# Blank rows written job by job, a last scatter pinned ahead of a loop, and input loads moved to ACT's queue: a scan and mixture-of-experts kernel

## The chip, the cores and the metric

The kernel runs on one core of one Trainium2 chip. The metric is device time in microseconds (us) for one execution of the whole program; lower is better. Engines are named as the profile names them: PE (TensorE matmul), PEld (its weight load), DVE (VectorE), ACT (ScalarE), POOL (GpSimd) and SP (SyncE); an added q (SPq, POOLq) is the engine's instruction queue.

## The reference

The input is x and f_logit of 4 sequences by 3648 steps by 256 channels. A gated scan comes first, then each of the 14592 tokens is routed to one of 16 experts and passes through its two matrices.

```python
sig = 1.0 / (1.0 + np.exp(-f_logit))
f = lower_bound + (1.0 - lower_bound) * sig
for t in range(S):
    h = f[:, t] * h + (1.0 - f[:, t]) * x[:, t]     # y[:, t] = h
g_idx = argmax(y @ w_group)                          # 4 groups
e_idx = argmax(y @ w_expert[g_idx])                  # 4 experts in each
ye = np.maximum(y @ w1[g, e], 0.0) @ w2[g, e]        # 256 -> 1024 -> 256
out[token] = g_w * e_w * ye                          # softmax weights of the two choices
```

## The kernel before, in words

**Phase 1** cuts the 14592 tokens into 29 units of 512. `p1_load` (L157) brings the inputs of a unit (tile `zt`, 1 MB, 4 buffers) from `in_zx_dram`, two units ahead (`AHEAD` = 3); all these loads stand on SP's queue (L169). `p1_ta` (L172) has ACT compute the gate (tanh at L179, scale and bias at L183), `p1_tb` (L187) has DVE run the scan into `h` (L196, L207), PE transposes `h` into rows (L226) and multiplies with the router's weights (L238), and ACT copies both out (`rows` at L228, `rs` at L241). `route_thunks` (L252) finds the expert of each token and its place in the expert's list for groups of two units; POOL then scatters the rows (L322, 114 indirect DMAs of 128 rows) into the DRAM tensor `xs`, which holds one list for each expert.

**Phase 2** is 32 jobs. Sixteen jobs of kind A take the first two to six tiles (128 tokens each) of every list as soon as these are filled (table `EARLY`); they run between the steps of phase 1. Sixteen of kind B take what is left of the lists, the longest list first; they start when all tokens are routed. A job loads its rows (`job_rows`, L592, tile `xr`, load at L607), its weights in four pieces of 512 KB (`job_weights`, L612, tile `st`, 5 buffers, L615), splits each weight into two halves of 16 bits (`job_split`, L618: ACT's cast at L621 makes `wh`, DVE's subtract at L622 makes `wl`), transposes the rows (L636), and runs two matrix products of three matmuls each (`m1_step`, L655, with ACT at L671 and DVE at L672 behind it; `m2_step`, L675). ACT scales the result by the token's weight (`o`, L687) and POOL scatters it to the output (L688, 123 indirect DMAs).

**The order of the work.** PE, ACT, DVE and POOL are ordered by a scheduler that goes through the program as it is written; SP is under `manual_schedule` (L707) and keeps the order of the text up to `in_order.close()` (L823). The main loop (L795) writes a job's steps and between them, through `bg_step` (L772), the steps of phase 1 and the preparation of the next job. `fetch_to` (L723) keeps the weight loads five pieces ahead. `order()` (L446) closes phase 1: it ranks what is left of the lists (`nord` rows from place `pord` on), and writes 256 blank rows behind each of the 16 lists (L486 to L489), so that a job that reads past the end of a list finds rows that belong to no token. Each blank write is a read of the place from the tile `taili` (L487) and a DMA of 258 KB (L488), all on SP's queue.

**The end.** Behind the last `m2_step` (L821) the count of tiles that did not fit the jobs is read (`left`, L824), and a loop of that many rounds does them (L825); in the execution shown here it makes no round (123 output scatters for the 55 and 68 tiles of the A and B jobs).

Of the kernel before, what the change touches and what calls it, by code (L numbers as in the profile page):

```python
# [15 lines left out]
ALU = mybir.AluOpType  # L16
AX = mybir.AxisListType.X

P = 128
NE = 16  # L20
# [12 lines left out]
O_BUFS = 5  # L33
X_BUFS = 4
AHEAD = 3


@with_exitstack
def gated_scan_moe(ctx: ExitStack, tc, zx, lower, wroute, wexp, out, S):
    nc = tc.nc  # L40
    sync = nc.sync
    ctx.enter_context(nc.allow_low_precision(reason="whole numbers small enough to be exact"))
    N, D = out.shape
# [3 lines left out]
    NT = N // P  # L47
    PRE = max(n for _, n in EARLY) * P
    LW = PRE + N + 2 * P
    LIST = NE * LW  # L50
    LROWS = LIST + 2 * P
    RW = D + 2

    xs = nc.dram_tensor("xs", [LROWS, RW], I32).ap()
# [45 lines left out]
    for u in sorted({u for u, _ in EARLY}):  # L100
# [4 lines left out]
                                scalar1=-1.0, scalar2=None, op0=ALU.add)  # L105
# [12 lines left out]
    blank = const.tile([P, RW], I32, name="blank")  # L118
# [19 lines left out]
    runoff = const.tile([P, NE], F32, name="runoff0")  # L138
    nc.vector.tensor_scalar(out=runoff, in0=eoff, scalar1=-1.0, scalar2=None, op0=ALU.add)
    state = {"runoff": runoff, "h": None}  # L140

    def unit_range(u):
        return u * UNIT, min(N, (u + 1) * UNIT)
# [11 lines left out]
    last_load = {}  # L155

    def p1_load(u):  # L157
        if u >= NU:
            return
        a, b = unit_range(u)  # L160
        w = b - a
        zt = p1.tile([P, 2, KD, UNIT], F32, name="zt", bufs=4)
        src = zx[u * P:(u + 1) * P, :].rearrange("p (s k w) -> p s k w", s=2, k=KD)
        if u == 0:
            for k in range(KD):
                for q in range(2):
                    nc.sync.dma_start(out=zt[:, q, k, 0:w], in_=src[:, q, k, 0:w])
        else:
            last_load[u] = nc.sync.dma_start(out=zt[:, :, :, 0:w], in_=src[:, :, :, 0:w])  # L169
        units[u] = {"z": zt}  # L170

    def p1_ta(u):  # L172
# [158 lines left out]
    def p1_thunks(us, groups):  # L331
# [21 lines left out]
        def put(f):  # L353
            th.append(f or (lambda: None))
            if hasattr(f, "mark"):
                marks[f.mark] = len(th)

        put(lambda: [p1_load(u) for u in range(us[0], us[0] + AHEAD - 1)])
        put(lambda: p1_ta(us[0]))
        for u in us + [us[-1] + 1]:  # L360
            seq = []
            if u in us:
                seq += [lambda u=u: (p1_load(u + AHEAD - 1), u + 1 in us and p1_ta(u + 1), early_blanks(u + 4))]
            if u - 1 in us:
# [78 lines left out]
    regs = {}  # L443
    early_loads = []

    def order():  # L446
        V = nc.vector
        run = const.tile([P, NE], F32, name="run")
# [20 lines left out]
        nord = const.tile([P, NE], F32, name="nord")  # L469
# [4 lines left out]
        pord = const.tile([P, NE], F32, name="pord")  # L474
# [7 lines left out]
        V.tensor_copy(ordi, eord)  # L482
        regs["ordi"] = ordi
        taili = const.tile([1, NE], I32, name="taili")
        V.tensor_scalar(out=taili, in0=state["runoff"][0:1], scalar1=1.0, scalar2=None, op0=ALU.add)
        for e in range(NE):  # L486
            r = sync.value_load(taili[0:1, e:e + 1], min_val=e * LW + PRE, max_val=e * LW + PRE + N)  # L487
            sync.dma_start(out=xs[bass.ds(r, 2 * P), :].rearrange("(p k) c -> p k c", k=2),  # L488
                           in_=blank[:, None, :].broadcast_to([P, 2, RW]))  # L489
        over = const.tile([P, NE], F32, name="over")  # L490
        V.scalar_tensor_tensor(out=over, in0=nord, scalar=63.5, in1=caps, op0=ALU.add, op1=ALU.subtract)
        V.tensor_scalar(out=over, in0=over, scalar1=1.0 / P, scalar2=None, op0=ALU.mult)
# [38 lines left out]
        left = const.tile([1, 1], F32, name="left")  # L531
# [60 lines left out]
    def job_rows(j):  # L592
        e = job_e(j)
        queue = sync
        if j.kind == "A":
            pos = queue.value_load(j.pos[0:1, e:e + 1], min_val=e * LW + PRE - j.tiles * P, max_val=e * LW + PRE)
        elif j.kind == "B":
            pos = sync.value_load(regs["pordi"][0:1, j.idx:j.idx + 1], min_val=0,
                                  max_val=(NE - 1) * LW + 2 * PRE)
        else:  # L600
            pos = sync.value_load(regs["tabs"][0:1, 3 * j.idx + 1:3 * j.idx + 2], min_val=0, max_val=LIST)
        if j.kind != "A":
            job_mask(j)
        j.rows, j.meta = [], []
        for t0, m in j.pieces:
            r = mo.tile([P, 2, RW], I32, name="xr", bufs=XR_BUFS)
            ld = queue.dma_start(out=r[0:j.w, 0:m], in_=xs[bass.ds(pos + t0 * j.w, m * j.w), :].rearrange("(p k) c -> p k c", k=m))  # L607
            if j.kind == "A":
                early_loads.append(ld.ins)
            j.rows.append(r)  # L610
# [95 lines left out]
    in_order = ExitStack()  # L706
# [12 lines left out]
    def bg_to(n):  # L719
        while done[0] < n:  # L720
            bg_pop()
# [28 lines left out]
    def start_macro(mi):  # L750
        mac = macros[mi]
        bg_to(marks[EARLY[mac[0].idx][0]] if mac[0].kind == "A" else marks["order"])
        for j in mac:
            if j.kind != "A":
                job_rows(j)

    def work(mac):
        return sum(len(j.chunks) * KF + j.tiles for j in mac)
# [36 lines left out]
    for mi, mac in enumerate(macros):  # L795
# [5 lines left out]
        left = sum(len(j.chunks) * KF + j.tiles for j in mac)  # L801
# [15 lines left out]
        while q:  # L817
            q.popleft()()
    pj, pc = pending
    for t in range(pj.chunks[pc][1]):  # L820
        m2_step(pj, pc, t)  # L821

    in_order.close()  # L823
    left = nc.values_load(regs["left"][0:1, 0:1], min_val=0, max_val=NT)  # L824
    with tc.For_i(0, left, 1) as it:  # L825
        ent = mo.tile([1, 3], I32, name="ent")
        rem = mo.tile([P, 1], F32, name="rem")
# [2 lines left out]
        j = make_job("X", 0)  # L830
# [54 lines left out]
```

## Time and profile before

| | us |
|---|---|
| median of 3 runs | 883.24 |
| the 3 runs | 876.09, 883.24, 884.25 |
| the profiled execution, its own time | 878.25 |
| its span, first to last instruction | 876.5 |

PE is busy for 753.8 us of the span (86%), DVE for 535.7, ACT for 464.2, POOL for 286.9. The span falls into three parts: up to about 411 us phase 1 and the A jobs run together; from 421 us on the B jobs run alone; the last 10 us close the program. "Granted clock" is the share of TensorE's full clock that the chip allowed in a stretch. A number in brackets behind an instruction is the time that its engine was idle ahead of it, with the instruction or transfer that ended the wait.

### The profile page before, as it was taken

Reading aid. Unit: us, or ns where it says so; the run is one execution under the profiler, and the core shown is the slowest. Engines: PE = TensorE matmul, PEld = TensorE weight load, DVE = VectorE, ACT = ScalarE, POOL = GpSimd, SP = SyncE. Lnnn points to the kernel's source line nnn. Section 1 sums busy time; section 2 is a strip of 40 time slices with the busy share of each in tenths; the row PEclk is TensorE's granted clock in tenths of the full one; section 3 lists DMA queues with packets and bytes.
Section 4 is the critical chain, followed back from the end, with each engine's and each line's share of the span. In section 5 each row is a group of like instructions: output and inputs, shape, how many; then the busy total and the mean of one; then the engine's idle time right before and its main releaser. Section 6 shows DMA issues by size and latency. Waiting matters only on the chain.

```text
span 876.5 us, 17542 instructions
## 1 busy us (share of the span) xinstructions
PE 753.8 (86%) x6629; PEld 646.5 (74%) x6629; DVE 535.7 (61%) x1159; ACT 464.2 (53%) x808; POOL 286.9 (33%) x255
## 2 busy tenths in 40 slices
PE   3452869878887888897799999999999999999995
PEld 2231748756676776766599998999888999999895
DVE  7996959888965953672534454543656445555630
ACT  6763949588745644342545444544555445555531
POOL 0484554734634425541121121212221221112122
PEclk9665979979999989999799999999999999999998
DMA  8993999799897244247641632343543424444300
GB/s 309 273 362 124 304 295 360 225 354 323 279 255 256 101 162 161 100 163 200 223 151 43 217 105 71 105 129 90 144 138 98 122 94 150 146 151 135 126 24 22
DMA packets 59056, 155.34 MB, mean 177 GB/s; under 512 B 11179, under 2 KB 24560, under 8 KB 55515
## 3 DMA queue, kind: packets, MB, share of 16 engines
q1 hardware_dynamic: 44443, 124.12, 44.3%
q0 software_dynamic: 14240, 30.06, 9.8%
q8 instruction: 52, 0.85, 0.4%
q14 instruction: 33, 0.27, 0.1%
q10 hardware_dynamic: 288, 0.03, 0.0%
HBM read 112.65 MB, written 42.05 MB: 176 GB/s over the span
## 4 chain that ended last, share of the span: by engine, by line
PE 56%; issue 11%; DVE 9%; DMA 7%; ACT 4%; SPq 2%; POOL 2%; POOLq 0%; another core or an unknown queue 0%; DVEq 0%; ACTq 0%
PE ps_m L683 9%; PE ps_m L681 9%; PE ps_m L682 9%; PE ps_m L666 8%; PE ps_m L668 8%; PE ps_m L667 8%; DMA st<-in_wexp_dram 5%; DVE wl L622 3%; PE ps_p L636 2%; DVE hl L672 2%; ACT wh L621 2%; POOL out_dram L688 1%; SPq L488 1%; PE ps_p L238 1%; DVE h L207 1%
## 5 line engine op out<-in xcount | busy, mean ns | idle before, releaser
L688 POOL DMA_INDIRECT out_dram<-o,meta x123 | 140.9, 1146 | 472.9 <-ACT o L687 441.2
L681 PE MATMUL ps_m<-wh,hh 128*128 128x256 f16 (+6 forms) x984 | 272.6, 277 | 2.0 <-ACT o L687 1.1
L682 PE MATMUL ps_m<-wl,hh 128*128 128x256 bf16 (+6 forms) x984 | 272.4, 277 | 0.8 <-issue 0.8
L683 PE MATMUL ps_m<-wh,hl 128*128 128x256 f16 (+6 forms) x984 | 272.2, 277 | 0.9 <-issue 0.9
L666 PE MATMUL ps_m<-xh,wh 128*128 128x256 f16 (+12 forms) x896 | 252.7, 283 | 19.8 <-DVE hl L672 19.3
L672 DVE SCALAR_TENSOR_TENSOR hl<-ps_m,hh 128x512 bf16<-128x512 f32 (+11 forms) x270 | 166.1, 620 | 168.7 <-ACT hh L671 128.2
L668 PE MATMUL ps_m<-xh,wl 128*128 128x256 f16 (+12 forms) x896 | 252.4, 283 | 0.2 <-issue 0.2
L667 PE MATMUL ps_m<-xl,wh 128*128 128x256 bf16 (+12 forms) x896 | 252.4, 283 | 0.0
L671 ACT ACTIVATE hh<-ps_m 128x512 f16<-128x512 f32 (+11 forms) x270 | 146.7, 546 | 129.2 <-PE ps_m L668 112.1
L622 DVE TENSOR_TENSOR wl<-st,wh 128x1024 bf16<-128x1024 f32 x128 | 155.4, 1219 | 57.7 <-ACT wh L621 57.5
L322 POOL DMA_INDIRECT xs<-rows,posi x114 | 143.8, 1262 | 110.6 <-issue 27.7
L621 ACT CAST wh<-st 128x1024 f16<-128x1024 f32 x128 | 132.8, 1044 | 43.3 <-DMA st<-in_wexp_dram 22.8
L687 ACT ACTIVATE o<-ps_m,meta 128x256 f32<-128x256 f32 (+6 forms) x123 | 58.3, 474 | 159.5 <-PE ps_m L683 137.7
L681 PEld LDWEIGHTS <-hh 128*128 128x128 f16 (+6 forms) x984 | 112.5, 114 | 12.0 <-issue 4.1
L683 PEld LDWEIGHTS <-hl 128*128 128x128 bf16 (+6 forms) x984 | 112.4, 114 | 10.1 <-issue 2.3
L682 PEld LDWEIGHTS <-hh 128*128 128x128 f16 (+6 forms) x984 | 112.5, 114 | 9.4 <-issue 1.4
L667 PEld LDWEIGHTS <-wh 128*128 128x128 f16 x896 | 88.9, 99 | 38.0 <-issue 22.7
L666 PEld LDWEIGHTS <-wh 128*128 128x128 f16 x896 | 89.0, 99 | 19.1 <-issue 2.7
L668 PEld LDWEIGHTS <-wl 128*128 128x128 bf16 x896 | 88.8, 99 | 19.1 <-issue 1.7
L642 DVE TENSOR_TENSOR xl<-ps_p,xh 128x512 bf16<-128x512 f32 (+9 forms) x68 | 41.9, 617 | 65.1 <-ACT xh L641 64.5
L207 DVE TENSOR_TENSOR_SCAN h<-zt,h 128x512 f32<-128x512 f32 (+4 forms) x56 | 65.1, 1170 | 1.6 <-PE ps_p L226 1.4
L636 PE MATMUL ps_p<-ident,xr 128*128 128x128 f32 (+6 forms) x246 | 40.0, 284 | 30.0 <-DMA xr<-xs 22.0
(120 smaller groups left out, 506.4 us busy)
## 6 DMA issues: line engine op xcount, KB each, us to landing
st<-in_wexp_dram SPq DMA_DIRECT2D x128, 512.0 KB
zt<-in_zx_dram SPq DMA_DIRECT2D x27, 1024.0 KB
xr<-xs SPq DMA_DIRECT2D x31, 258.0 KB
xs<-blank SPq DMA_DIRECT2D x22, 258.0 KB
xr<-xs SPq DMA_DIRECT2D x8, 249.9 KB
out_dram<-o,meta POOLq DMA_INDIRECT x123
xs<-rows,posi POOLq DMA_INDIRECT x114
xs<-blank SPq DMA_DIRECT2D x3, 516.0 KB
```

Of the source, the lines that this page charges most:

```text
L322: sc = nc.gpsimd.indirect_dma_start(out=xs_v[G["t0"] + t][:, :], out_offset=bass.IndirectOffsetOnAxis(ap=R["posi"][:, t:t + 1], axis=0), i ...
L621: nc.scalar.copy(j.wh[i], j.st[i])
L622: nc.vector.tensor_tensor(out=j.wl[i], in0=j.st[i], in1=j.wh[i], op=ALU.subtract)
L666: nc.tensor.matmul(po, w1_at(j.wh, k, c), xh[:, k], start=(k == 0), stop=False)
L667: nc.tensor.matmul(po, w1_at(j.wh, k, c), xl[:, k], start=False, stop=False)
L668: nc.tensor.matmul(po, w1_at(j.wl, k, c), xh[:, k], start=False, stop=(k == KD - 1))
L671: nc.scalar.activation(hi, pv, AF.Relu)
L672: nc.vector.scalar_tensor_tensor(out=j.hl[ch][:, cs[0]:cs[-1] + 1, 0:w], in0=pv, scalar=0.0, in1=hi, op0=ALU.max, op1=ALU.subtract)
L681: nc.tensor.matmul(pm[0:p, 0:D], j.hh[ch][:, c, ts], w2_at(j.wh, c), start=(c == 0), stop=False)
L682: nc.tensor.matmul(pm[0:p, 0:D], j.hh[ch][:, c, ts], w2_at(j.wl, c), start=False, stop=False)
L683: nc.tensor.matmul(pm[0:p, 0:D], j.hl[ch][:, c, ts], w2_at(j.wh, c), start=False, stop=(c == KF - 1))
L688: nc.gpsimd.indirect_dma_start(out=out_v[out_n[0]][:, :], out_offset=bass.IndirectOffsetOnAxis(ap=lt[0:p, r, 0:1], axis=0), in_=o[0:p], in ...
```

## The change

There are three edits. The blank rows behind list number 0 (in the order of the B jobs) are written in `order()`; those of list s + 1 are written by `start_macro` right behind the row loads of B job s, and the place comes from `pord` + `nord` in place of `runoff` + 1. From unit 9 on the input loads are issued from ACT's queue. POOL keeps the order of the text from the last `m2_step` on, and the read of `left` stands inside that stretch.

```diff
+ZX_SP = 9
...
-            last_load[u] = nc.sync.dma_start(out=zt[:, :, :, 0:w], in_=src[:, :, :, 0:w])
+            last_load[u] = (nc.sync if u < ZX_SP else nc.scalar).dma_start(out=zt[:, :, :, 0:w], in_=src[:, :, :, 0:w])
...
+    def tail_blank(s):
+        r = sync.value_load(regs["taili"][0:1, s:s + 1], min_val=PRE, max_val=(NE - 1) * LW + PRE + N)
+        sync.dma_start(out=xs[bass.ds(r, 2 * P), :].rearrange("(p k) c -> p k c", k=2),
+                       in_=blank[:, None, :].broadcast_to([P, 2, RW]))
...
-        V.tensor_scalar(out=taili, in0=state["runoff"][0:1], scalar1=1.0, scalar2=None, op0=ALU.add)
-        for e in range(NE):
-            r = sync.value_load(taili[0:1, e:e + 1], min_val=e * LW + PRE, max_val=e * LW + PRE + N)
-            sync.dma_start(out=xs[bass.ds(r, 2 * P), :].rearrange("(p k) c -> p k c", k=2),
-                           in_=blank[:, None, :].broadcast_to([P, 2, RW]))
+        V.tensor_tensor(out=taili, in0=pord[0:1], in1=nord[0:1], op=ALU.add)
+        regs["taili"] = taili
+        tail_blank(0)
...
             if j.kind != "A":
                 job_rows(j)
+                if j.kind == "B" and j.idx + 1 < NE:
+                    tail_blank(j.idx + 1)
...
     pj, pc = pending
+    in_order.enter_context(tc.manual_schedule(engines={mybir.EngineType.Pool}))
     for t in range(pj.chunks[pc][1]):
         m2_step(pj, pc, t)
-
+    left = nc.values_load(regs["left"][0:1, 0:1], min_val=0, max_val=NT)
     in_order.close()
-    left = nc.values_load(regs["left"][0:1, 0:1], min_val=0, max_val=NT)
```

The first place is SP's queue at `order()`. Before, it ends with the last of the sixteen blank writes (`taili` read, DMA from `blank`), the table for the leftovers (`tab`), and then the weight loads of the next job (`st`):

```order
L487 TENSOR_LOAD taili
L487 ISA x2
L488 ISA
L488 DMA xs<-blank 256x1x258
L522 DMA tab<-resi 128x3
L615 DMA st<-in_wexp_dram 128x1024 x4
L574 TENSOR_LOAD ordi
```

In the changed kernel the same place (its lines are some numbers further down) reads, from the last row load of an A job on:

```order
L611 DMA xr<-xs 128x516
L448 TENSOR_LOAD taili
L448 ISA x2
L449 ISA
L449 DMA xs<-blank 256x1x258
L526 DMA tab<-resi 128x3
L619 DMA st<-in_wexp_dram 128x1024 x4
L578 TENSOR_LOAD ordi
```

One blank write is left of sixteen. The other fifteen stand further down, each between the row loads of one B job and the weight loads that follow, as here:

```order
L611 DMA xr<-xs 124x258
L448 TENSOR_LOAD taili
L448 ISA x2
L449 ISA
L449 DMA xs<-blank 256x1x258
L578 TENSOR_LOAD ordi
L578 ISA x2
L619 ISA
L619 DMA st<-in_wexp_dram 128x1024
```

The second place is ACT's queue in the middle of phase 1, about 170 to 190 us into the program before. The rows before are the tanh of unit 19 with what stands around it (`zt` a unit's input, `hh` the first product of a job, `rs` and `rows` copies for the router):

```order
L621 CAST wh_2279<-st 128x1024
L687 ACTIVATE o<-ps_m_2213,meta 128x256
L228 COPY rows<-ps_p 128x2x256
L179 ACTIVATE zt<-zt 128x1024
L671 ACTIVATE hh<-ps_m_2256 128x2x256
L183 ACTIVATE zt<-zt,mid,half 128x512 x2
L671 ACTIVATE hh<-ps_m_2295 128x2x256
L621 CAST wh_2312<-st 128x1024
L241 COPY rs<-ps_p 128x128
```

The same tanh in the changed kernel:

```order
L691 ACTIVATE o<-ps_m_2177,meta 128x256
L170 DMA zt<-in_zx_dram 128x2048
L180 ACTIVATE zt<-zt 128x1024
L691 ACTIVATE o<-ps_m_2213,meta 128x256
L184 ACTIVATE zt<-zt,mid,half 128x512 x2
L229 COPY rows<-ps_p 128x2x256
L675 ACTIVATE hh<-ps_m_2256 128x2x256
L625 CAST wh_2273<-st 128x1024
L625 CAST wh_2279<-st 128x1024
```

The load now stands ahead of the tanh of the unit before it, and there is one such pair for each unit; the casts of the weights have moved behind the tanh.

The third place is the end of POOL's queue. Before, the last output scatter stands behind the loop (the one at the third row is the loop's own):

```order
L825 UNCONDITIONAL_BRANCH
L881 BRANCH_PREFETCH_HINT
L688 DMA out_dram<-o,meta 14592x256
L825 REGISTER_ALU
L825 COMPARE_AND_BRANCH
L825 UNCONDITIONAL_BRANCH
L688 DMA out_dram<-o,meta 14592x256
L881 UNCONDITIONAL_BRANCH
L881 ISA
```

Now only the loop's own scatter is left there, and the run of scatters ahead of the read of `left` has 91 in place of 90:

```order
L692 DMA out_dram<-o,meta 14592x256 x91
L829 TENSOR_LOAD lefti
L831 COMPARE_AND_BRANCH
L831 ISA
L831 UNCONDITIONAL_BRANCH
L831 ISA
L831 UNCONDITIONAL_BRANCH
L887 BRANCH_PREFETCH_HINT
L692 DMA out_dram<-o,meta 14592x256
L831 REGISTER_ALU
L831 COMPARE_AND_BRANCH
L831 UNCONDITIONAL_BRANCH
```

## Rows read from the trace of the kernel before

**Rows 1.** Stage, length, busy us of PE, PEld, DVE, ACT, POOL, granted clock, DMA

```profile
160.00:250.00 90.00, 74.94 (x613) 56.49 (x611) 78.91 (x156) 62.99 (x111) 44.37 (x35) 0.92 0.92 304
250.00:300.00 50.00, 38.92 (x356) 32.41 (x355) 33.09 (x71) 29.14 (x53) 20.70 (x16) 0.93 0.68 204
411.00:421.00 10.00, 0.16 (x2) 0.00 (x0) 1.64 (x3) 2.72 (x5) 0.00 (x0) 0.76 0.90 239
421.00:427.00 6.00, 5.89 (x23) 3.05 (x23) 4.08 (x7) 3.27 (x6) 0.00 (x0) 0.55 0.76 264
427.00:866.00 439.00, 437.68 (x3970) 400.22 (x3968) 221.56 (x385) 211.94 (x366) 95.28 (x84) 1.00 0.37 116
```

**Rows 2.** Timeline of ACT and PE behind the order step (start, length, idle before)

```profile
418.28 1.04 ACT L621 CAST wh<-st 128x1024 f16<-128x1024 f32 x1 [9.75 <-DMA st<-in_wexp_dram]
421.11 0.48 PE L666 MATMUL ps_m<-xh,wh 128*128 128x384 f16 x1 [9.94 <-DVE hl L672]
```

**Rows 3.** Timeline of SP's queue around the order step

```profile
384.44 3.93 SPq L607 DMA_DIRECT2D xr<-xs  x6
389.19 20.96 SPq L488 DMA_DIRECT2D xs<-blank  x16
410.90 15.00 SPq L615 DMA_DIRECT2D st<-in_wexp_dram  x8
```

**Rows 4.** Chain that ended last: two transfers (start, length)

```profile
111.86 2.48 DMA xr<-xs
...
864.46 3.63 DMA out_dram<-o,meta
```

**Rows 5.** Timeline of SP's queue: two input loads, with what stands ahead of one

```profile
161.05 1.84 SPq L607 DMA_DIRECT2D xr<-xs  x2
163.89 0.42 SPq L169 DMA_DIRECT2D zt<-in_zx_dram  x1
...
262.79 0.42 SPq L169 DMA_DIRECT2D zt<-in_zx_dram  x1
```

**Rows 6.** Timeline of ACT: three tanh steps that waited for their input load

```profile
175.34 1.06 ACT L179 ACTIVATE zt<-zt 128x1024 f32<-128x1024 f32 x1 [3.68 <-DMA zt<-in_zx_dram]
271.13 1.06 ACT L179 ACTIVATE zt<-zt 128x1024 f32<-128x1024 f32 x1 [4.07 <-DMA zt<-in_zx_dram]
281.74 1.06 ACT L179 ACTIVATE zt<-zt 128x1024 f32<-128x1024 f32 x1 [6.35 <-DMA zt<-in_zx_dram]
```

**Rows 7.** Timeline of PE: three gaps between 170 and 290 us

```profile
181.54 0.69 PE L636 MATMUL ps_p<-ident,xr 128*128 128x128 f32 x2 [8.05 <-ACT rs L241]
266.01 0.48 PE L249 MATMUL ps_p<-ident,rs 128*128 128x128 f32 x1 [4.62 <-ACT rs L241]
286.26 0.19 PE L284 MATMUL ps_p<-scn,tri 128*128 128x16 bf16 x1 [4.02 <-DVE xl L642]
```

**Rows 8.** What SP's queue waited for: total us, times, longest; and L169's waits

```profile
SPq L615 <- DVE wl L622: 256.6, 53, 16.3
SPq L607 <- DMA xs<-rows,posi: 53.3, 12, 9.8
SPq L169 <- DVE h L207: 25.7, 6, 5.8
...
L169 SPq EVENT_SEMAPHORE  x11: 17/3426/5729, 5.2 to 47.8; - x11
```

**Rows 9.** Two stretches of the first half, columns as in rows 1

```profile
155.00:161.00 6.00, 6.00 (x68) 5.19 (x67) 6.00 (x16) 4.74 (x8) 4.78 (x5) 1.00 0.23 83
165.00:210.00 45.00, 35.83 (x300) 27.41 (x298) 36.26 (x71) 30.74 (x52) 25.34 (x21) 0.89 1.01 345
```

**Rows 10.** The end: timeline of ACT and POOL; instructions of the closing line

```profile
866.31 0.47 ACT L687 ACTIVATE o<-ps_m,meta 128x256 f32<-128x256 f32 x1 [2.15 <-PEq L825]
869.96 1.00 POOL L688 DMA_INDIRECT out_dram<-o,meta  x1 [4.32 <-issue]
...
L881 POOLq DRAIN  x3: 40/109/5956, 869.7 to 876.2; - x3
```

## The prediction

> **What bounds the kernel now.** I first read busy time by stage. From 427 to 866 us PE is busy for 437.68 of 439.00 us at a granted clock of 1.00 [rows 1]: the B jobs are bound by PE, and nothing that SP, ACT or POOL does there can shorten them; it can only move their start and lengthen the close behind them. So a gain must come from ahead of 427 us or from the last 10 us. Ahead of it PE has room: 74.94 of 90.00 us from 160 on, 38.92 of 50.00 from 250 on, and 0.16 of 10.00 from 411 on [rows 1].
>
> Then I read who ends these gaps. The one at 411 us is plain: PE waits 9.94 us behind DVE's `hl`, but ACT, ahead of DVE, sat 9.75 us with a weight cast that waited for its `st` load [rows 2]. SP issued that load only at 410.90, because sixteen blank writes held its queue for 20.96 us from 389.19 on [rows 3]. It landed 7.4 us later, when the cast began.
>
> The gaps between 170 and 290 us are less plain. Three of them, 8.05, 4.62 and 4.02 us, end on ACT's `rs` and on DVE [rows 7]. ACT stood still shortly ahead of each, at the tanh of a unit whose input had not landed: 3.68, 4.07 and 6.35 us [rows 6]. These inputs are loads that SP issued late. That of unit 19 went out at 163.89, behind a row load of 161.05 [rows 5], and SP's row loads wait for scatters for 53.3 us in all [rows 8]. It was used at 175.34 [rows 6], 11.5 us later; that of unit 26, out at 262.79 [rows 5], at 271.13 [rows 6], 8.3 us later.
>
> The end comes last: the last `o` is done at 866.78 (866.31 and 0.47), but POOL's scatter of it starts at 869.96 [rows 10], behind the empty loop.
>
> **The change part by part: blank rows.** Sixteen writes take 20.96 us, 1.31 us each [rows 3]; fifteen leave this place, 19.65 us. That would let the `st` load go at 391.25. The one write that stays is a write at a place known only at run time, so it has to wait for the six row loads in front of it. The last of those is out at 388.37 (384.44 and 3.93) [rows 3], and a row load took 2.48 us to land [rows 4], so the write goes at 390.9 in place of 389.19 and the load at about 393.0. With the 7.4 us of before it lands at 400.4. ACT asks for it at 408.53 (418.28 less 9.75) [rows 2], so 8.1 us of margin are left and the whole gap of 9.94 us goes.
>
> What is behind the gap goes too. From 421 to 427 us the granted clock was 0.55, after 10 us in which PE had done nothing; from 427 on it was 1.00 [rows 1]. The work of those 6.0 us takes 6.0 x 0.55 = 3.3 us at the upper level (2.4 GHz, against 1.2): 2.7 us. Together 12.6 us. Bounds: 8 us if a later load, say that of the next weights, keeps a third of the gap; 12.6 if nothing does.
>
> The fifteen writes come back among the B jobs. Each costs SP about 1.3 us and a wait until the row loads of its job have landed, 2.5 us by rows 4 and at most the 9.8 us of the longest wait for `xs` [rows 8]. Behind it on SP stand the weight loads of a later job. They are early: SP waited 256.6 us in 53 pieces, 4.8 us each, only for a staging buffer to come free [rows 8], and PE hardly waited from 427 on [rows 1]. I cost this at 0. With that cover gone it would be 15 x 3.8 = 57 us of SP time, which PE would see in part; four such waits, one for each weight piece of a job, are 19 us, so the cover holds even for 1.3 + 9.8 us.
>
> **The pinned scatter.** Now it starts about 0.3 us behind ACT, as other scatters do, at 867.1 in place of 869.96 [rows 10]: 2.9 us earlier. The loop's entry must then wait for it to land, 3.63 us as for the scatter before it [rows 4], 870.7. In the old order POOL went from that landing at 868.09 (864.46 and 3.63) to its closing drain at 869.7, 1.6 us later, and the drain took 5.96 us with the scatter inside, to 875.7 [rows 10]. The new close is thus 870.7 + 1.6 + a drain + 0.8 us (the span ends at 876.5). With an empty drain that is 873.1, a gain of 3.4 us; with a drain as long as before it is 879.1, a loss of 2.6. The nearer row is the drain with work in it, which should shorten once there is none: I take a gain of 3.0, and keep -2.6 to 3.4.
>
> **Input loads from ACT.** Twenty loads (units 9 to 28) leave SP's queue. Each now stands one unit ahead on ACT. Units 19 and 26 are seven apart and their tanhs 95.8 us [rows 6], so a load has some 13.7 us to land where it took 8.3 to 11.5: the three waits of 14.1 us [rows 6] mostly go. Behind them lie PE gaps of 8.05 + 4.62 + 4.02 = 16.7 us [rows 7]. I take half, 8 us, for three reasons: an issue costs its queue about 0.42 us [rows 5], so ACT pays 20 x 0.42 = 8.4 us, in a stretch where DVE is busy for 78.91 of 90.00 us [rows 1] and can't follow a faster PE far; the scatters that SP waited for stay where they are; and the weight loads still stand behind them. Bounds: 20 us (all three gaps and some 3 us of low clock behind them) and -4 us (no gap goes, half of the 8.4 us is seen).
>
> Can the DMA engines take the loads earlier at all? From 165 to 210 us they are busy for 1.01 of the time and a load moved there gains nothing; from 155 to 161 us, while SP waits, for only 0.23 [rows 9]. The Trainium skill, "DMA: Bandwidth & Descriptors", section "Issuing engines are not separate DMA queues", says that transfers of all issuing engines share the same 16 DMA engines and that a second issuer saves only the time of issuing, which is usually small. By that rule alone the edit would be worth about the 8.4 us of SP issue, none of it on PE's path, and the sum would be 862.7; the trace agrees on the sharing (1.01), but shows that an issue here can also be stuck behind a wait.
>
> **The sum**, against the profiled execution's own 878.25: 878.25 - 12.6 - 3.0 - 8.0 = 854.7. That execution lies 5.0 us under the median of the three runs shown, 883.24; the mean of all four is 880.5, 2.2 us above it. I add that: 857 us.
>
> **Rivals.** *The transfer is hidden anyway.* The DMA engines are the limit up to 250 us (0.92 from 160 on [rows 1]), so loads that go out earlier only slow the weight loads beside them, and the first half keeps its length. For it speaks 1.01 [rows 9], against it the 0.23 and the share of 0.68 from 250 on [rows 1], where two of the three waits lie. Then only blanks and end count: 878.25 - 15.6 = 862.7, with the 2.2 about 865.
>
> *ACT takes over SP's waits* (the slower side). SP waited 25.7 us in 6 pieces for DVE to free an input buffer, 4.3 us each [rows 8]. On ACT such a wait holds the casts, the Relu of the first product and the scaled outputs behind it, so PE and DVE stand too. Were each of the sixteen loads from unit 13 on held for 4.3 us and half of it seen by PE, that is 34 us: 878.25 - 15.6 + 34 = 897. It decides from 15.6 / 2.15 = 7 such waits on; from there the kernel is slower than before. Against it: SP's waits of this line all began by 47.8 us [rows 8], while the first units were loaded as fast as buffers came free; on the later loads, which the change moves, there was none.
>
> **How the numbers follow.** My forecast has a chance of 0.60; hidden transfers 0.22; ACT's waits 0.10; 0.08 is left for more than the forecast, when the first half gives back all three gaps and more. The range: from 843 (12.6 + 3.4 + 20 = 36 us off 878.25, 842.3, rounded up) to 874 (8 us from the blanks, -2.6 from the end, -1 from the loads: 878.25 - 4.4). A measurement of this kernel tells about 1% from no change, 8.8 us around 883.24. Forecast, hidden transfers and the surplus, 0.90 in all, lie below 874.4; I take 0.09 off for the case that the low bounds come together (8 - 2.6 - 4 = 1.4 us), which leaves 0.81 for faster. These 0.09 and a mild case of ACT's waits, 0.02, are 0.11 for the same; 0.08 is slower.
>
> **What would show it.** In the profile of the changed kernel PE should have no gap of more than 1 us where the A jobs pass into the B jobs, and the granted clock should stay at 1.00 there; the first `st` load behind `order()` should go out within 5 us of the last row load. In the B jobs PE should be busy as before and SP should show short waits in front of fifteen blank writes. ACT's waits for `zt` from 100 us on should fall from more than 14 us to under 5, and the B jobs should start about 20 us earlier than 427. The last scatter should start within 0.5 us of the last `o`. I am wrong if ACT shows waits at its own load instructions, if PE's gap at the passage is there with another name, or if the stage ahead of `order()` is as long as before.

## The result, and the profile after it

The changed kernel takes 852.17 us (median of four runs, 851.39 to 855.85), the kernel before 880.28 us beside it: a ratio of 0.967, with a 95% interval of 0.964 to 0.971. The prediction was 857 us, 843 to 874. The profiled execution of the changed kernel is the slowest of its four, 855.85 us with a span of 853.4.

A first word on names. The text ahead of the prediction, and the prediction, call the stretch behind 421 us "the B jobs". That is wrong: phase 1 ends there, but the last A jobs go on. The first output block of a B job (the 56th of all, and the first of 124 rows) starts on ACT at 521.31 us before and at 498.64 us now. What the prediction calls the passage from A to B lies inside the job A13 (A0 to A15 are the jobs of kind A, the early jobs). Lines of the changed kernel stand 1 to 6 numbers further down.

The stages of the changed kernel (columns as in rows 1):

```profile
160.00:250.00 90.00, 84.67 (x734) 63.73 (x733) 84.39 (x178) 67.45 (x124) 48.31 (x39) 0.98 0.97 318
250.00:300.00 50.00, 48.47 (x469) 41.96 (x468) 44.70 (x89) 34.37 (x61) 27.78 (x22) 1.00 0.64 215
300.00:376.00 76.00, 63.77 (x512) 50.41 (x510) 42.38 (x145) 30.15 (x58) 34.69 (x32) 0.91 0.44 143
376.00:385.00 9.00, 0.35 (x2) 0.25 (x2) 2.23 (x3) 3.31 (x5) 0.00 (x0) 0.68 0.81 265
385.00:391.00 6.00, 6.00 (x37) 4.46 (x35) 2.62 (x4) 0.75 (x2) 0.00 (x0) 0.63 0.56 203
391.00:843.00 452.00, 450.53 (x4070) 410.07 (x4069) 227.46 (x396) 219.36 (x379) 97.84 (x87) 1.00 0.40 122
```

Against [rows 1] the first half is much fuller: PE 84.67 us in place of 74.94 from 160 on, 48.47 in place of 38.92 from 250 on. But the empty stage is still there, now from 376 us on, and so is the low granted clock behind it (0.63, so in part at 1.2 GHz, the lower level). Here is what stands around it, first SP's queue, then ACT and PE (start, length, idle before):

```profile
363.72 4.23 SPq L611 DMA_DIRECT2D xr<-xs  x6
371.94 0.61 SPq L449 DMA_DIRECT2D xs<-blank  x1
372.64 0.55 SPq L526 DMA_DIRECT2D tab<-resi  x1
373.24 12.84 SPq L619 DMA_DIRECT2D st<-in_wexp_dram  x7
```

```profile
371.96 0.48 ACT L691 ACTIVATE o<-ps_m,meta 128x256 f32<-128x256 f32 x1 [2.19 <-PE ps_m L687]
381.69 1.05 ACT L625 CAST wh<-st 128x1024 f16<-128x1024 f32 x1 [9.26 <-DMA st<-in_wexp_dram]
382.64 0.59 ACT L675 ACTIVATE hh<-ps_m 128x512 f16<-128x512 f32 x1
...
384.65 0.37 PE L670 MATMUL ps_m<-xh,wh 128*128 128x256 f16 x1 [8.85 <-DVE hl L676]
```

One blank write stands where sixteen stood [rows 3], and the weight load goes out 5.3 us behind the last row load (373.24, against 363.72 and 4.23). All the same ACT waits 9.26 us for it and PE 8.85, where it was 9.75 and 9.94 [rows 2].

Where the time came from is best read by work, not by time: the starts of the 123 output activations `o` (one for each output block), which come in the same order in both kernels.

| output block | before, us | after, us | after is ahead by |
|---|---|---|---|
| 1 | 117.9 | 123.3 | -5.4 |
| 25 | 317.4 | 288.5 | 28.9 |
| 34 | 390.9 | 369.3 | 21.6 |
| 40 | 433.7 | 411.1 | 22.7 |
| 123 | 866.3 | 843.6 | 22.7 |

The lead grows up to block 25, loses 7 us up to block 34, and gains only 1.1 us across the gap. From block 40 on it doesn't move. The spans differ by 23.1 us, so the close of the program gave 0.4.

What ACT waited for from 100 to 345 us, in total us, times and longest, before:

```profile
ACT zt L179 <- DMA zt<-in_zx_dram: 18.3, 5, 6.3
...
ACT wh L621 <- DMA st<-in_wexp_dram: 10.5, 4, 6.3
```

and after:

```profile
ACT wh L625 <- DMA st<-in_wexp_dram: 10.9, 2, 8.7
...
ACT zt L180 <- DMA zt<-in_zx_dram: 2.1, 1, 2.1
```

The waits for inputs went from 18.3 to 2.1 us. Those for weights stayed, and 8.7 us of them are now one wait, at 302.82 us, between blocks 25 and 34, where the lead is lost: it is 21.1 us at block 26, right behind that wait. That is not all of the loss, for at block 28 the lead is back at 26.0 us. It falls again to 21.7 us at block 30, where ACT waits 5.12 us at 317.55 and 2.46 us at 322.74 for something that the view calls "remote", a sender that it can't name (more on these waits at the end). SP's own waits grew (those for `xs` were 53.3 us [rows 8]; L449 is the blank write):

```profile
SPq L611 <- DMA xs<-rows,posi: 88.4, 12, 23.0
SPq L449 <- DMA xr<-xs: 59.1, 17, 11.2
```

And the end of the changed kernel (rows 10 show it before; the drain's three lengths are its shortest, median and longest, in ns, then the first and last start):

```profile
843.65 0.47 ACT L691 ACTIVATE o<-ps_m,meta 128x256 f32<-128x256 f32 x1 [2.15 <-PEq L831]
844.40 1.00 POOL L692 DMA_INDIRECT out_dram<-o,meta  x1 [1.43 <-ACT o L691]
...
L887 POOLq DRAIN  x3: 40/103/4722, 847.9 to 853.2; - x3
```

The scatter now starts 0.28 us behind the end of `o`, 3 us earlier than before. The span still ends 9.75 us after the start of the last `o` (853.4 less 843.65), where it was 10.19 (876.5 less 866.31).

The total came out near the forecast, but not its parts. The runs below ask which part of the change is worth what, and why the gap is still there.

### The profile page after: what moved, and what is told of

Same layout as the page of the kernel before. It is cut to its first block, busy times and chain, and to the rows that moved or that the text cites. A ratio compares the mean times of both kernels' runs of the same rounds, so it can differ in the third digit from the quotient of the medians.

```text
span 853.4 us, 17549 instructions
## 1 busy us (share of the span) xinstructions
PE 749.6 (88%) x6629; PEld 642.8 (75%) x6629; DVE 540.9 (63%) x1159; ACT 461.3 (54%) x808; POOL 283.9 (33%) x255
## 4 chain that ended last, share of the span: by engine, by line
PE 56%; issue 15%; DVE 14%; DMA 6%; ACT 4%; POOL 3%; SPq 0%; POOLq 0%; another core or an unknown queue 0%; DVEq 0%; ACTq 0%
PE ps_m L687 9%; PE ps_m L685 9%; PE ps_m L686 9%; PE ps_m L670 8%; PE ps_m L672 8%; PE ps_m L671 8%; DVE h L208 3%; DVE wl L626 3%; DMA xs<-rows,posi 2%; PE ps_p L640 2%; DVE zt L197 2%; POOL out_dram L692 2%; POOL xs L323 2%; DMA st<-in_wexp_dram 2%; DVE hl L676 2%
## 5 line engine op out<-in xcount | busy, mean ns | idle before, releaser
L323 POOL DMA_INDIRECT xs<-rows,posi x114 | 140.7, 1234 | 130.9 <-issue 27.9
L227 PE MATMUL ps_p<-ident,h 128*128 128x128 f32 x228 | 45.1, 328 | 12.1 <-DVE h L208 11.5
```

Of the source, the lines that this page charges most:

```text
L323: sc = nc.gpsimd.indirect_dma_start(out=xs_v[G["t0"] + t][:, :], out_offset=bass.IndirectOffsetOnAxis(ap=R["posi"][:, t:t + 1], axis=0), i ...
```

## The experiments

The runs came in groups, not all on one chip. The same kernel before took 880 and 882 us beside the first two groups and 862 and 864 beside the two later ones, on other chips. So times are compared inside a group, and across groups only ratios to the kernel before.

### One part undone at a time

Each of the first three kernels is the changed one with one part undone: the blank writes in one place again, all input loads on SP again, the end unpinned.

```diff
 # blank writes in one place (in order())
...
-        tail_blank(0)
...
+        for e in range(NE):
+            r = sync.value_load(taili[0:1, e:e + 1], min_val=e * LW + PRE, max_val=e * LW + PRE + N)
+            sync.dma_start(out=xs[bass.ds(r, 2 * P), :]...
...
-                if j.kind == "B" and j.idx + 1 < NE:
-                    tail_blank(j.idx + 1)
 # loads on SP
-ZX_SP = 9
+ZX_SP = 99
 # end not pinned
-    in_order.enter_context(tc.manual_schedule(engines={mybir.EngineType.Pool}))
...
+    in_order.close()
     left = nc.values_load(regs["left"][0:1, 0:1], min_val=0, max_val=NT)
-    in_order.close()
```

Expected of the run with the blank writes in one place:

> The changed kernel with the sixteen blank writes put back to one place behind the last row loads; loads from ACT and the pinned end stay. Additive theory (each part is worth its own term of the prediction): 12.6 us above the changed kernel, about 865 us. Interaction theory (the loads from ACT bring TensorE to the passage earlier than the stuck queue can serve it, so every blank write in front of the weight loads counts in full): the first weight load behind them moves from 373.24 to about 393, TensorE's gap there grows from 8.85 to 26 to 30 us, about 872 us.

Expected of the run with the loads on SP:

> The changed kernel with all input loads issued by SP again; blanks job by job and the pinned end stay. Additive theory: 8 us above the changed kernel, about 860 us. Interaction theory: TensorE loses the whole 21.6 us that it was ahead at 345 us, but its gap of 8.85 us at the passage goes too, since it comes there late enough for the weights: about 13 to 15 us above, 865 to 867 us, with no TensorE gap over 2 us between 370 and 430 us.

Expected of the run without the pinned end:

> The changed kernel with the order of the last scatter left to the scheduler and the loop's bound read before the last output rows. Additive theory: 3 us above the changed kernel, about 855 us, as the last scatter would start some 3 us after the last output activation again. Rival (the closing drain on POOL takes its 4.7 to 6 us from the last work on whatever queue): 0 to 0.5 us above, 852 to 852.7 us.

Measured, beside 882.47 us of the kernel before on the same chip:

| kernel | median, us | ratio, interval | ahead of before at block 25, 34, 40, 123 |
|---|---|---|---|
| blanks in one place | 853.69 | 0.968 [0.963, 0.973] | 32.5, 29.8, 26.0, 26.0 |
| loads on SP | 873.71 | 0.989 [0.983, 0.994] | 2.8, 2.2, 3.0, 3.0 |
| end not pinned | 852.07 | 0.965 [0.958, 0.971] | 28.5, 18.3, 25.0, 25.0 |

Three findings. **The loads carry nearly everything:** with them back on SP the ratio goes from 0.967 to 0.989, some 19 us (21.6 us above the unpinned run on the same chip), and the lead at block 25 from 28.9 to 2.8. ACT's waits for inputs are back:

```profile
ACT zt L180 <- DMA zt<-in_zx_dram: 21.2, 5, 9.9
ACT wh L625 <- DMA st<-in_wexp_dram: 12.6, 8, 4.6
```

(The view of above, for the run with the loads on SP.) **The pinned end is worth nothing that can be measured.** Unpinned, the last `o` starts at 841.33, its scatter at 844.99 as before the change, and the span ends at 851.5, 10.2 us behind `o`. The closing drain then takes 5.97 us, from 3.5 us behind the start of `o` on; with the pin it takes 4.72 us, from 4.3 us on:

```profile
L887 POOLq DRAIN  x3: 40/109/5966, 844.8 to 851.3; - x3
```

**The blank writes in one place cost nearly nothing**, where both theories wanted 12 to 20 us. This was the surprise, and neither theory held. Its trace has all sixteen writes in front of the weight loads, and a longer gap:

```profile
358.08 4.22 SPq L613 DMA_DIRECT2D xr<-xs  x6
363.19 21.41 SPq L494 DMA_DIRECT2D xs<-blank  x16
...
385.33 15.27 SPq L621 DMA_DIRECT2D st<-in_wexp_dram  x8
```

```profile
392.97 1.04 ACT L627 CAST wh<-st 128x1024 f16<-128x1024 f32 x1 [14.19 <-DMA st<-in_wexp_dram]
...
395.79 0.48 PE L672 MATMUL ps_m<-xh,wh 128*128 128x384 f16 x1 [14.38 <-DVE hl L678]
```

The gap of 14.38 us lies behind output block 38. In the changed kernel the gap of 8.85 us lies ahead of block 36. And the run with the loads on SP has one too, of 9.59 us at 404.87, again ahead of block 36: there the blank writes were moved, TensorE was late, and the gap that this edit was to close is still there. So the edit does not only move loads on SP. What else it moves is seen in ACT's order, which nobody wrote by hand. The rows around the cast, with the blanks in one place (the kernel before has the same order of kinds here):

```
L693 ACTIVATE o<-ps_m_5432,meta 128x256
L677 ACTIVATE hh<-ps_m_5464 128x2x256
L677 ACTIVATE hh<-ps_m_5485 128x2x256
L677 ACTIVATE hh<-ps_m_5506 128x2x256
L677 ACTIVATE hh<-ps_m_5527 128x2x256
L693 ACTIVATE o<-ps_m_5548,meta 128x256
L647 CAST xh<-ps_p 128x2x256
L693 ACTIVATE o<-ps_m_5589,meta 128x256
L647 CAST xh<-ps_p 128x2x256
L693 ACTIVATE o<-ps_m_5630,meta 128x256
L647 CAST xh<-ps_p 128x2x256
L627 CAST wh_5833<-st 128x1024
```

and in the changed kernel, from the same `o` (block 35) on:

```
L691 ACTIVATE o<-ps_m_5282,meta 128x256
L625 CAST wh_5683<-st 128x1024
L675 ACTIVATE hh<-ps_m_5314 128x2x256
L625 CAST wh_5704<-st 128x1024
L675 ACTIVATE hh<-ps_m_5335 128x2x256
L675 ACTIVATE hh<-ps_m_5356 128x2x256
L675 ACTIVATE hh<-ps_m_5377 128x2x256
L691 ACTIVATE o<-ps_m_5398,meta 128x256
```

The cast is the 61st, the first of job A15. With fewer blank writes ahead of its load on SP the scheduler puts it four Relus (`hh`) and three output blocks earlier. The Relus behind it belong to A13. TensorE has A13 and A14 still ahead of it and doesn't need A15's weights for them: A15's first output block, the 50th, leaves only at 466.2 us. But ACT takes its instructions one by one, so A13's Relu waits behind a cast for a job that is two jobs away, and TensorE waits for the Relu. The Trainium skill, "PSUM — Partial Sum Buffer", section "Engine vs sequencer instructions", says that ScalarE's queue is strictly first in, first out. The trace agrees: the Relu at 382.64 starts when the cast does its last 0.1 us, after 9.26 us in which its product was long done.

### Is it SP's order, or ACT's?

Two edits tell it apart. The first leaves the scheduler free and has the weight loads of the last early jobs go ahead of the row loads that wait for scatters.

```diff
+ROWS_LATE = (27,)            # and (23, 25, 27), and (11, 13, ... 27)
...
-                    f = lambda u=u: early_rows(u)
+                    f = (lambda: None) if u in ROWS_LATE else (lambda u=u: early_rows(u))
...
+        if j.kind == "A" and EARLY[j.idx][0] in ROWS_LATE:
+            def rows():
+                job_rows(j)
+                if j.idx == NE - 1:
+                    bg_to(marks["order"])
+                    tail_blank(0)
+                    regs["close"]()          # the write of tab
+            th.append(rows)                  # behind the four weight pieces
```

> The changed kernel with the row loads of the last two early jobs, the first blank write and the leftover table put behind the weight loads of their own job in SP's queue. Theory (the gap of 8.85 us at the passage is SP's order: four weight loads that need nothing stand behind row loads that wait for the last scatters): the gap falls below 2 us, its low clock behind it goes too, 8 to 11 us below the changed kernel, about 842 us. Rival (TensorE would wait there in any case, for the rows themselves, which no order brings before the last scatter's landing at 363.7 us): within 2 us of the changed kernel, with the gap's releaser the transposes of rows in place of the weights.

Measured on the chip of the first three: 844.04 us, ratio 0.957 [0.952, 0.962], 8 us below the changed kernel (and below the unpinned run beside it, which differs from it by nothing that can be measured). SP's queue now issues A15's four weight loads with A14's, in one run of eight, ahead of the row loads that wait for scatters:

```profile
318.65 1.66 SPq L611 DMA_DIRECT2D xr<-xs  x3
320.42 35.52 SPq L619 DMA_DIRECT2D st<-in_wexp_dram  x8
360.74 1.43 SPq L611 DMA_DIRECT2D xr<-xs  x3
363.05 20.75 SPq L619 DMA_DIRECT2D st<-in_wexp_dram  x4
384.65 1.80 SPq L611 DMA_DIRECT2D xr<-xs  x3
```

No gap over 1.4 us is left behind 346 us, and the lead goes from 24.6 at block 34 to 37.0 at block 40. The rows were not what TensorE was short of.

The second edit leaves SP's order as it is and holds back only the casts of A15. They take a scale of 1.0 that DVE works out from the last Relu of A13, so that the scheduler cannot put them ahead of it:

```diff
-        nc.scalar.copy(j.wh[i], j.st[i])
+        if j.kind == "A" and j.idx == NE - 1:
+            nc.scalar.activation(j.wh[i], j.st[i], AF.Copy, scale=regs["gate"][:, 0:1])
+        else:
+            nc.scalar.copy(j.wh[i], j.st[i])
...
+        if j.kind == "A" and j.idx == NE - 3 and ch == 1 and cs[-1] == KF - 1:
+            regs["gate"] = const.tile([P, 1], F32, name="gate")
+            nc.vector.tensor_scalar(out=regs["gate"], in0=hi[:, len(cs) - 1, 0:1], scalar1=0.0, scalar2=1.0,
+                                    op0=ALU.mult, op1=ALU.add)
```

> The changed kernel with the weight casts of the last early job held back on ACT by a scale of 1.0 that is worked out from the last Relu output of the job two before it; SP's order is that of the changed kernel. Theory (the gap of 8.85 us is ACT's order: TensorE has two jobs of work that don't need these weights, but their Relu stands behind the cast): the casts come some 25 us of TensorE work later, the gap falls below 2 us, 8 to 11 us below the changed kernel, 841 to 844 us, as in the run that moved the weight loads on SP. Rival (TensorE itself is out of work until the weights land): the gap comes back behind the later casts, within 2 us of the changed kernel, 852.

It took 822.90 us on a chip where the kernel before took 862.09, a ratio of 0.955 [0.950, 0.961]. The absolute number I had named was for the chip before (and so are those for the three other runs of this group, which come further down), so the edit was run again, with the changed kernel and the one with the blanks in one place beside it.

> The changed kernel itself, unaltered, as the mark for the three others on this chip. It should stand at 0.964 to 0.971 of the kernel before, as when it was first timed, with a TensorE gap of 4 to 9 us ahead of the 36th output block.

> The sixteen blank writes in one place again, on the same chip as the changed kernel. If ACT's order is what the blank edit is paid back with (the two casts stand three output blocks earlier in the changed kernel), it is 0 to 3 us above the changed kernel, with a TensorE gap of 12 to 16 us behind the 36th output block. Rival (the first comparison was blurred by the chip): 8 us above or more.

> The gate on the casts of the last early job, on the same chip as the changed kernel: 8 to 12 us below it, without a TensorE gap over 2 us behind 350 us. Rival (the low time of the first run with the gate was that chip's): within 3 us of the changed kernel.

| kernel, on one chip | median, us | ratio, interval | ahead of before's profile at block 25, 34, 40, 123 |
|---|---|---|---|
| before | 863.77 | | |
| changed | 835.16 | 0.967 [0.964, 0.971] | 35.1, 43.9, 44.9, 44.9 |
| changed, blanks in one place | 838.78 | 0.971 [0.967, 0.974] | 35.4, 44.6, 39.3, 39.3 |
| changed, one gate | 822.92 | 0.952 [0.948, 0.956] | 36.2, 43.1, 54.4, 54.4 |
| changed, four gates (below) | 819.01 | 0.948 [0.944, 0.952] | 35.8, 46.8, 59.0, 58.3 |

(The profile of before is from another chip. What counts in the last column is the difference between rows and between blocks.) Up to block 34 the first three changed kernels agree to 1.5 us; what sets them apart lies between blocks 34 and 40. The cast and TensorE's gap, in the changed kernel:

```profile
360.23 1.04 ACT L625 CAST wh<-st 128x1024 f16<-128x1024 f32 x1 [10.04 <-DMA st<-in_wexp_dram]
...
363.19 0.37 PE L670 MATMUL ps_m<-xh,wh 128*128 128x256 f16 x1 [9.63 <-DVE hl L676]
```

with the blanks in one place:

```profile
379.22 1.04 ACT L627 CAST wh<-st 128x1024 f16<-128x1024 f32 x1 [15.29 <-DMA st<-in_wexp_dram]
...
382.05 0.48 PE L672 MATMUL ps_m<-xh,wh 128*128 128x384 f16 x1 [15.48 <-DVE hl L678]
```

and with one gate, where the cast waits for the gate and not for the load:

```profile
373.84 2.19 ACT L626 ACTIVATE wh<-st,gate 128x1024 f16<-128x1024 f32 x2 [0.69 <-DVE gate L683]
```

That gives the blank edit's account. Moving the fifteen writes brings the load to ACT 19.0 us earlier (360.23 against 379.22). But ACT also asks for it 13.7 us earlier (at 350.19, 360.23 less 10.04, against 363.93), with just that much work of A13 left undone behind the cast. What is left is 5.3 us of shorter wait, 5.6 us of lead, and 3.6 us between the medians, whose intervals overlap. With the gate the same loads land in time for a cast that stands where it is needed, and 12.2 us are gained (9.5 us of lead between the two profiled executions). All three runs came out a little over what I had named for them (a gap of up to 9 us, 0 to 3 us for the blanks, 8 to 12 for the gate). The gap was ACT's order together with SP's; changing either alone removes it.

### The other wait, and how far the cure goes

The wait of 8.68 us at 302.82 us is also that of a cast for a load which SP issued behind row loads that waited for scatters. The first try was the edit on SP for more jobs.

> As the run that put the row loads of the last two early jobs behind their weight loads (844.0 us), with the same done for the two jobs before them. Theory (the cast that waits 8.68 us at 302.82 us has the same cause: its load, issued at 296.91, stands behind row loads that wait for scatters until 295.52): that wait falls below 2 us, and TensorE keeps most of the 7 us of lead that it loses between 290 and 345 us in the changed kernel, 836 to 840 us. Rival (in that stretch the lists that the scatters write are what TensorE is short of, so the wait changes its name only): 842 to 846 us.

> The same for every early job from the fifth on. Before the twelfth job the only waits of a cast for its load are of 2.2 us at 177.52, so by the theory it is worth at most 2 us more than the run with four jobs: 834 to 840 us. Rival (a job's rows come later, and the transposes that open the next job wait for them): TensorE gets gaps behind row loads of 1 to 3 us a job in ten jobs, 845 us or more.

With four jobs (A12 to A15) the run took 825.45 us, ratio 0.958 [0.953, 0.963] against 0.957 for two: no gain. The cast's wait is gone, but the transposes of the rows wait in its place (2.88 us at 309.67, then 1.61 and 1.47):

```profile
309.67 0.66 PE L640 MATMUL ps_p<-ident,xr 128*128 128x128 f32 x2 [2.88 <-DMA xr<-xs]
```

From the fifth early job on it is a clear loss: 897.86 us, ratio 1.041 [1.035, 1.047], 4% slower than the kernel before. TensorE waits for rows twelve times (the 16.1 us are the first rows of all, a wait that the other kernels have too):

```profile
PE ps_p L640 <- DMA xr<-xs: 91.5, 12, 16.1
```

Up to A11 the rows are what a job waits for, and a row load must stand ahead of the weights. For the last two jobs it is the other way round; with the two before them added it made no difference. The rival that I had set at 1 to 3 us a job was right in kind, with eight gaps of 7 to 13 us.

The second try was the gate on ACT for the last four early jobs, with SP's order untouched.

> The same gate on the casts of the last four early jobs, each held until the last Relu of the job two before it. With the gate on one job ACT still waits 8.55 us at 295.83 and 6.01 us at 321.82 for weight loads behind row loads. If those waits hold TensorE, they go, and the time is 4 to 8 us below the run with one gate. Rival (TensorE has no other work there, or the casts now come too late for their own job): within 2 us of one gate, or above it, with gaps behind the casts' low halves.

819.01 us, 3.9 us below one gate, just under what I had named. With one gate ACT still had two waits:

```profile
295.47 1.04 ACT L628 CAST wh<-st 128x1024 f16<-128x1024 f32 x1 [8.64 <-DMA st<-in_wexp_dram]
...
322.23 1.04 ACT L628 CAST wh<-st 128x1024 f16<-128x1024 f32 x1 [5.11 <-DMA st<-in_wexp_dram]
```

With four there is no wait of a cast for a load over 2.6 us from 100 us on, and PE is busy for 94.26 us of the stretch from 250 to 345, in place of 91.20. Of the 13.75 us that ACT waited there TensorE can have seen only some 4: it was idle for 3.8 us of the stretch, and the gates gave 3.1 us of them back. This is the best kernel of the study, 5.2% below the kernel before and 16 us below the changed one.

### Input loads from the first unit on

The last run takes the slower rival by its word: the first nine units, for which SP waits until DVE frees a buffer, also go to ACT (`ZX_SP = 0`).

> The changed kernel with every input load issued by ACT, the first nine units too, for which SP waited 25.7 us in 6 pieces until DVE freed an input buffer. Theory (such a wait on ACT holds only what stands behind it there, and ACT has little to do before 60 us): within 3 us of the changed kernel. Rival of the prediction (ACT takes over SP's waits, half of them seen by TensorE): the first output activation comes 10 us or more later than at 123 us, and the time is 860 to 866 us.

840.29 us, ratio 0.976 [0.970, 0.981], against 0.967 [0.964, 0.971] for the changed kernel: some 7 us worse, but the intervals touch, and the changed kernel itself was not run on this chip. The first output block starts at 127.7 us, against 121.5 in the changed kernel on another chip and 121.1 to 121.7 in the three other runs on this one, so the mechanism of the rival is there, at a size between the two expectations. In the first 85 us ACT waits 13.9 us for inputs, where it was 3.8 in the changed kernel:

```profile
ACT zt L180 <- DMA zt<-in_zx_dram: 10.0, 3, 7.0
...
ACT zt L183 <- DMA zt<-in_zx_dram: 3.9, 2, 2.9
```

Which instruction held the early loads back on ACT was not traced further.

## Why the prediction was right in total and wrong in its terms

**The bound.** From 391 us on PE is busy for 450.53 of 452 us, and block 40 to block 123 take 432.6 us before and after. All of the gain but 0.4 us lies ahead of that, as predicted, and the fifteen blank writes that came back among the B jobs cost TensorE nothing. I had put their waits and their own time on SP at 57 us together; the waits alone were 59.1 us. The cover holds all the same.

**Blank rows, 12.6 us: measured 3.6, beside the new loads.** The step that failed is "ACT asks for it at 408.53, so 8.1 us of margin are left and the whole gap of 9.94 us goes". SP's side of it came as said: one write, waiting for the row loads to land, and the weight load right behind. But I took the time at which ACT asks from the trace of before and held it fixed. It hangs on the same edit: the scheduler that writes ACT's order put the cast 13.7 us of work earlier once its load came earlier, and ate 13.7 of the 19.0 us. I had compared the two orders of ACT in the middle of phase 1 and not here, where the term rested; these are the rows in the ordinary fences above. The prediction named the sign of this, "PE's gap at the passage is there with another name", and it was: 8.85 us behind the same load.

**Input loads, 8 us with bounds of -4 and 20: measured about 19.** The step that failed is "I take half". Of its three reasons the first two fell. The issue cost ACT 0.33 us a load, 6.7 us for twenty, but with no wait at them that the profile shows, and DVE did follow: 84.39 of 90 us from 160 on, against 78.91. The third held and took nothing off the gain that can be seen: SP waited longer for scatters than before (88.4 us for 53.3 [rows 8]) and ACT as long for weights. And the three PE gaps were not the measure: the waits of ACT's tanh fell by 16.2 us from 100 to 345 us, and TensorE's clock rose with its work (0.92 to 0.98 from 160 on [rows 1]). The total of 18.3 us that ACT waited for inputs, which stood in the trace before, is nearer to what was measured; I read three of the waits and halved what I saw behind them. One of the three was also misread. TensorE's gap that ends at 266.01 [rows 7] was over when the tanh's wait began at 267.06 [rows 6], so it can't come of it; ahead of it stands a weight cast that waited:

```profile
260.08 2.94 ACT L621 CAST wh<-st 128x1024 f16<-128x1024 f32 x3 [6.29 <-DMA st<-in_wexp_dram]
```

That the gain came by the inputs, and not by what else got free on SP's queue, is argued: no run parts the two. ACT's waits for weights from 100 to 345 us, 10.5 before and 10.9 after, speak against the second.

**The pinned scatter, 3.0 us: measured 0.4 in the spans, and nothing between the medians.** The scatter starts when I said. The step that failed is that "an empty drain" is short. Without the scatter in it the drain still takes 4.72 us, and ends 9.0 us behind the start of the last `o`, against 9.4 us unpinned. What the 4.72 us consist of stays open.

**The sum.** 23.6 us were forecast and 28.1 measured, because a term that was 9 us too large and one that was 11 too small nearly cancelled. That is luck, not a proof of the reasons. The parts are not simply additive either. Measured one by one they come to some 23 us, 5 less than the whole, and with the loads on SP the other two edits together gave 8.8 us between the medians (882.47 to 873.71), beside the new loads the blanks gave 3.6.

**The rivals.** *The transfer is hidden anyway* falls with the run that put the loads back: it is 19 us slower. By the Trainium skill's rule, which the prediction weighed ("DMA: Bandwidth & Descriptors", section "Issuing engines are not separate DMA queues"), only the time of issuing is saved. The trace agrees on the shared engines, 0.97 busy from 160 to 250 us, but not on the price. The loads had stood behind SP's other waits, that of unit 19 behind row loads that waited 11.1 us for scatters, and that of unit 26 behind weight loads that waited 10.7 us for a transfer of weights, and leaving that queue was worth more than twice the issue time of 8.4 us. *ACT takes over SP's waits* did not happen at units 9 and on, as no wait for a buffer was there; it did, mildly, for the first nine.

## What to carry to other kernels

An edit that makes a transfer earlier can move the instruction that waits for it: where a scheduler writes the order of an engine, compare the order of that engine at the very instruction that your term rests on, before and after. When an engine waits, ask for whose work: here the idle 9 us were those of a cast that was needed two jobs later, and holding the cast back gained 12.2 us where bringing its load forward gained 3.6. Sum the waits of an engine over a stage before you put a price on three of them, and ask of each what it held up: 16.2 us less of tanh waits went with some 19 us of time here, but of 13.75 us of cast waits TensorE saw at most some 4.

## What the hardware showed that was not expected

The same program differs between chips, and nearly all of it in one stage. The changed kernel takes 852.17 us on one chip and 835.16 on another; from block 40 to block 123 its two profiles take 432.6 us each, from block 1 to block 34 246.0 and 225.6. The traces narrow these 20.4 us down. In that stretch ACT has seven waits on a "remote" sender in the first profile, 17.1 us in all, and none in the second. The three longest:

```profile
317.55 0.47 ACT L691 ACTIVATE o<-ps_m,meta 128x256 f32<-128x256 f32 x1 [5.12 <-remote]
322.74 0.27 ACT L242 COPY rs<-ps_p 128x128 f32<-128x128 f32 x1 [2.46 <-remote]
346.61 0.60 ACT L675 ACTIVATE hh<-ps_m 128x512 f16<-128x512 f32 x1 [3.99 <-remote]
```

The second profile pulls ahead where these stand, by 7.5 us from block 27 to 29 and by as much from block 31 to 33. Every profile of the first two groups has such waits, the kernel before too, and none of the two later groups has one. What ACT waited for there, and why only in these groups, stays open.

The closing drain on POOL: 5.97 us with the last scatter waiting inside it, 4.72 us with none. Taking work off the last queue shortened the program by 0.4 us, not by the 3 us by which the work came earlier.
